# Attention with an MLP behind it: constant bias rows by broadcast DMA, norms put between units, pair loads moved by a slot

## The chip, the cores and the metric

The kernel runs on one core of a Trainium2 chip. A core has TensorE (PE, matmuls), VectorE (DVE), ScalarE (ACT), GpSimd (POOL) and SyncE (SP, which only issues transfers). The metric is the device time of one execution in microseconds, lower is better; it is given as the median of several executions.

## What is computed

Two stages, for 8 batches of 8 heads, 576 positions and head dimension 64:

```python
# attention, per batch and head
cum    = cumsum(max(s, 0))
scores = q @ k.T / 8 + min(-(cum[i] - cum[j]), 0)      # -1e9 above the diagonal
attn_out = softmax(scores) @ v
# the heads side by side give x: [8, 576, 512]
xn  = (x - mean(x)) / sqrt(var(x) + 1e-6) * g_ln
out = x + max(xn @ w_ch1, 0) @ w_ch2                   # 512 -> 2048 -> 512
```

## The kernel before

All instructions stand in one order written out by hand; each engine goes through its own in that order. The main loop runs over the 64 heads, n = 8b + h. `pre(n)` issues loads and casts for later heads. `scores(b, h)` makes the transposed scores of one head in three PSUM banks and ACT's exponentials of them into `er`; `scores_d` does the last 64 keys for two heads at once. `pv_next()` takes the head that is two behind (`pend`) and does `pv`: 15 matmuls into `pot`, then DVE's `rinv`, the product into `xb` and that for the last 64 positions into `xm` (lines 360 to 369).

**Bias as extra rows.** k and q of four heads lie transposed in `kq[i]`, 64 rows of data and four more (rows D to KA): q carries c_hi and three rows of ones, k carries a row of minus ones and c_hi, c_mid, c_lo (`c3`, the scaled cumulative sum in three bf16 pieces). So the score matmul adds the bias. `aug(gam, ...)` writes the c rows of one group of four heads by four small DMAs from `c3` (L197, L199). The constant rows are filled by ACT, POOL and DVE (L538, L552, L608, L611). For head 0 the rows come from small matmuls `ba`, `bb` (L581, L585), since they are needed first.

**How k and q get there.** For the first three batches `qk_pair(g)` transposes pairs of heads on TensorE (L229) and copies them to `kq` by two copies for k and two for q. Pairs come by `ld_cast_pair` (POOL's DMA queue, which casts), or, for pairs 0 and 1, by `ld_pair` on SP and a cast. From batch 3 on, rows are cast by POOL and transposed by DMA. v of a batch comes in five tiles (`ld_v` on SP, `cast_v` on POOL).

**Norm and MLP.** When the last head of a batch has gone through `pv_next`, `ln_aggr`, `ln_xn` (L410, four or five tiles `xn`) and `ln_rstd` follow at once; two heads later `ln_tr` transposes the tiles into `xT` (L426, copy L431). The MLP of a batch is 32 units in a queue: 16 of `mlp1` (512 columns of hidden, four matmuls L439, and a Relu on ACT L449 or DVE L447) and four times four of `mlp2` (four matmuls L457 each; after the fourth, DVE makes `yo`, L466, which SP stores). `run_units(k)` puts k of them between the attention of the heads, so that TensorE has work while ACT and DVE are busy. The last 64 positions of all batches are gathered in `xm`, `xTm` and go through the MLP at the end (`mixed_units`). `keep_warm(k)` puts k matmuls on zeros where TensorE would be idle.

**Pools.** PSUM: `ps_s` three banks for scores, `ps_m` two for units and the first six pairs, `ps_t` two for transposes, later pairs and `scores_d`, `ps_o` one for `pot`. In SBUF, `pairs` holds four pairs, `stage` six tiles of loaded float32.

Of the kernel before, what the change touches and what calls it, by code (L numbers as in the profile page):

```python
# [19 lines left out]
def kernel(  # L20
# [70 lines left out]
    ones = const.tile([BH, S], BF16, name="ones")  # L91
    pick = const.tile([BH, 4, P], BF16, name="pick")
# [107 lines left out]

    def bias_rows():
        tr = ps_t.tile([P, 3, NT, BH], BF16, name="trc", tag="tr")
        for j, src in enumerate((c_hi, c_mid, c_lo)):
            for t in range(NT):
                pn = P if t < NF else TL
                nc.tensor.transpose(
                    tr[0:pn, j, t, :], src[:, t * P : t * P + pn], ident[0:BH, 0:BH]
                )
        for t0, t1, pn in ((0, NF, P), (NF, NT, TL)):
            nc.vector.tensor_copy(  # L210
                out=cT[0:pn, t0:t1, 0, :, 1:4],
                in_=tr[0:pn, :, t0:t1, :].rearrange("p j t x -> p t x j"),
            )
            nc.vector.tensor_copy(out=cT[0:pn, t0:t1, 1, :, 0], in_=tr[0:pn, 0, t0:t1, :])


    def qk_pair(g, k_eng, q_eng):
        b, j = g // 4, g % 4
        i = (g // 2) % 2
        hh = (j % 2) * 2  # L220
        for x, (kind, eng) in enumerate((("k", k_eng), ("q", q_eng))):
            src = ready.pop((kind, g))
            if g < 6:
                tr = ps_m.tile([P, S], BF16, name="trqk", tag="m")
            else:
                tr = ps_t.tile([P, S], BF16, name="trqk", tag="tr")
            for t in range(QT):

                nc.tensor.transpose(  # L229
                    tr[:, t * QP : (t + 1) * QP],  # L230
                    src[0:QP].rearrange("p h c -> p (h c)")[:, t * P : (t + 1) * P],
                    ident[0:QP, 0:QP],
                )
            dst = kq[i][0:D, x, hh : hh + 2, 0:S].rearrange(
                "d u (p r w) -> d u p r w", r=QT // 2, w=2
            )
            for w in range(2):
                copy_on(
                    eng,
                    dst[:, :, :, :, w],  # L240
                    tr[w * D : (w + 1) * D, :].rearrange("d (u r p) -> d u p r", u=2, p=QP),
                )
# [99 lines left out]
    def pv(b, h):  # L342
# [4 lines left out]
        pot = ps_o.tile([P, NT, D + 1], F32, name="pot", tag="pot")  # L347
# [46 lines left out]
    def ln_aggr(b):  # L394
        n = len(x_tiles(b))
        mvs[b] = small.tile([P, 5, 2], F32, name="mv", tag="mv", bufs=2)
        for t in range(n):
            nc.vector.bn_aggr(out=mvs[b][:, t, :], in_=st[b][:, t, :, :])
# [7 lines left out]
    def ln_xn(b):  # L406
        xTs[b] = xtp.tile([P, KD, 512], BF16, name="xT", tag="xT")
        for t, x in enumerate(x_tiles(b)):
            xn = xnp.tile([P, Dm], BF16, name="xn", tag="xn")
            nc.vector.scalar_tensor_tensor(  # L410
                out=xn,
                in0=x,
                scalar=mvs[b][:, t, 0:1],
                in1=gb,
                op0=ALU.subtract,
                op1=ALU.mult,
            )
            xns[b, t] = xn

    def ln_tr(b, t):  # L420
        if (b, t) not in xns:
            return
        xn = xns.pop((b, t))
        tr = ps_t.tile([P, KD, P], BF16, name="trx", tag="tr")
        for kd in range(KD):
            nc.tensor.transpose(tr[:, kd, :], xn[:, kd * P : (kd + 1) * P], ident)  # L426
        if t < NF:
            dst = xTs[b][:, :, t * P : (t + 1) * P]
        else:
            dst = xTm[:, :, (b // 2) * P : (b // 2 + 1) * P]  # L430
        nc.vector.tensor_copy(out=dst, in_=tr)  # L431
# [21 lines left out]
    def mlp2(t, quarter, x, rs, dst):  # L453
        if quarter == 0:
            py[0] = ps_m.tile([P, Dm], F32, name="py", tag="m")
        for fb in range(quarter * 4, quarter * 4 + 4):
            nc.tensor.matmul(  # L457
                py[0],
                lhsT=hT[:, fb, t * P : (t + 1) * P],
                rhs=w2_bf[:, fb, :],  # L460
                start=(fb == 0),
                stop=(fb == FB - 1),
            )
        if quarter == 3:
            yo = yop.tile([P, Dm], F32, name="yo", tag="yo")
            nc.vector.scalar_tensor_tensor(  # L466
                out=yo, in0=py[0], scalar=rs, in1=x, op0=ALU.mult, op1=ALU.add
            )
            dst(yo)


    def chunk_units(xT_of, of_t):
        units = [lambda fb=fb: mlp1(xT_of(), fb) for fb in range(FB)]
        for t in range(NF):
            for qr in range(4):
                units.append(lambda t=t, qr=qr: mlp2(t, qr, *of_t(t)))
        return units

    def batch_units(b):
        def of_t(t):  # L480
            def put(yo):
                nc.sync.dma_start(out=out[b, t * P : (t + 1) * P, :], in_=yo)
# [3 lines left out]
    def mixed_units():  # L486
        def of_t(t):
            def put(yo):
                nc.sync.dma_start(out=out[2 * t, NF * P : S, :], in_=yo[0:TL])
                nc.sync.dma_start(out=out[2 * t + 1, NF * P : S, :], in_=yo[TL:P])  # L490
            return xm[t], rstd[:, 2 * t + 1, NF:NT], put
        return chunk_units(lambda: xTm, of_t)
# [25 lines left out]
    for g in range(2):  # L518
        ld_pair("k", g)
        ld_pair("q", g)  # L520
    for t in range(3):
        ld_v(0, t)
# [9 lines left out]
    for j in range(3):  # L532
# [4 lines left out]
    nc.vector.memset(kq[0][0:KA, 0, :, S:SP], 0.0)  # L537
    nc.scalar.copy(  # L538
        out=kq[0][D:KA, 1, :, 0:S], in_=ones[0:4].unsqueeze(1).to_broadcast([4, G, S])
    )  # L540
# [11 lines left out]
    nc.gpsimd.memset(kq[0][D : D + 1, 0].bitcast(F32), NEG2)  # L552
    ld_cast_pair(2)
# [5 lines left out]

    nc.vector.tensor_scalar(  # L560
# [11 lines left out]
    aug(0, nc.sync, h0=1)  # L572
    ld_v(0, 3)
    qk_pair(0, "dve", "act")
# [3 lines left out]
    for j, src in ((3, ones), (0, c_hi), (1, c_mid), (2, c_lo)):  # L578
        if j == 2:
            keep_warm(4)  # L580
# [12 lines left out]
    cast_pair("k", 1, "pool")  # L593
    cast_pair("q", 1, "pool")
    ld_v(0, 4)
    ld_cast_pair(3)
    v_edges(0)
    for t in range(NT):
        cast_v(0, t, "pool")
    nc.gpsimd.memset(er[TL:P, :, OD : OD + TL], 0.0)  # L600
    nc.gpsimd.memset(er[:, :, OD + TL : EW], 0.0)


    def pre(n):
        if n == 0:
            nc.vector.memset(mhalf, -0.5)
            nc.vector.memset(kq[1][0:KA, 0, :, S:SP], 0.0)
            nc.vector.memset(kq[1][D : D + 1, 0].bitcast(F32), NEG2)  # L608
            ld_w1(0)
        elif n == 1:  # L610
            nc.vector.memset(kq[1][D:KA, 1].bitcast(F32), ONE2)  # L611
            aug(1, nc.sync)
            ld_cast_pair(4)
        elif n == 2:
            nc.sync.dma_start(out=gb, in_=moe_g_ln.partition_broadcast(P))
            ld_w1(1)
        elif n == 3:
            v_edges(1)
        elif n == 4:
            ld_w1(2)  # L620
        elif n == 5:
            ld_cast_pair(5)
        elif n == 6:
            ld_w1(3)
            ld_v(1, 0), ld_v(1, 1), ld_v(1, 2), ld_v(1, 3), ld_v(1, 4)
        elif n == 7:
            ld_w2(0)
        elif n == 8:
            ld_cast_pair(6)
            ld_w2(1)  # L630
            cast_v(1, 0, "pool")
            cast_v(1, 1, "pool")
        elif n == 9:
            ld_w2(2)
            cast_v(1, 2, "pool")
            cast_v(1, 3, "pool")
            cast_v(1, 4, "pool")
        elif n == 10:
            ld_cast_pair(7)
            ld_w2(3)  # L640
        elif n == 13:
            nc.vector.memset(cT[:, :, 0, :, 0], -1.0)
            nc.vector.memset(cT[:, :, 1, :, 1:4], 1.0)
            for r in rows:
                nc.gpsimd.memset(r[:, :, :, KA:P], 0.0)
        elif n == 14:
            bias_rows()

        for g in range(8, 4 * NPE):
            if n == 2 * g - 4:  # L650
                ld_cast_pair(g)
# [25 lines left out]
    NU = {n: 3 for n in range(12, 20)}  # L677

    def pv_next():
# [4 lines left out]
        if ph_ == 7:  # L684
            ln_aggr(pb)
            ln_xn(pb)
            ln_rstd(pb)


    for n in range(BH):  # L690
        b, h = n // H, n % H
        nu = NU.get(n, 4)
        pre(n)
        if n < 10:
# [3 lines left out]
            if n % 2 == 0 and n < 8:  # L698
                g = n // 2 + 1
                qk_pair(g, "dve", "act")  # L700
            if n < 8:
                keep_warm(2)
            if n == 9:
                for t in range(NF):
                    ln_tr(0, t)
                queue += batch_units(0)
            if n > 1 and n != 9:
                pv_next()
            if n == 8:
                pv_next()  # L710
                keep_warm(5)
                qk_pair(5, "act", "act")
            pend.append((b, h))
            continue
        if h % 2 == 1 and n + 1 < NPE * H:
            qk_pair((n + 1) // 2, "act" if h == 1 else "dve", "act")
        scores(b, h)
        run_units(1, True)
        if h % 2 == 0:
            scores_d(b, h // 2)  # L720
        run_units(1)
        pv_next()
        pend.append((b, h))
        lt = {2: (0, 1), 3: (2, 3, 4)}.get(h, ()) if b > 1 else ()
        for t in lt:
            ln_tr(b - 1, t)
            if t != 1 and t != 4:
                run_units(1)
                nu -= 1
        run_units(nu - 2)  # L730
        if b > 1 and h == 3:
            queue += batch_units(b - 1)
# [3 lines left out]
    run_units(5)  # L736
    for t in range(NT):
        ln_tr(B - 1, t)
        run_units(1)
# [33 lines left out]
```

The softmax here doesn't subtract the row's maximum and nothing guards it: scores larger than these inputs give would overflow.

## Time and profile before

| | |
|---|---|
| median of 3 runs | 387.54 us (386.29 to 388.04) |
| the profiled execution | 387.35 us, span 385.7 us |
| PE / DVE / ACT / POOL busy | 363.9 / 202.5 / 194.5 / 161.6 us |
| granted clock, mean | 0.98 |
| moved by DMA | 51.86 MB |
| the largest PE groups | py L457 137.9 us, ph L439 123.2, pot L352 40.6 |
| the idle matmuls of keep_warm | 39, busy 13.9 us |

The span is what the profiler saw between the first and the last instruction; 1.65 us of the execution lie around it. A matmul's end is modelled and runs into the next one, so a busy PE is read as "has work", and a stretch with less busy time than length as one with waits. The page's table of slices gives the busy share of 40 equal stretches of 9.6 us.

### The profile page before, as it was taken

How to read it: one execution, taken by the hardware profiler on the slowest of the kernel's cores; microseconds unless marked ns; L12 is line 12 of the kernel's file. 1: busy time of each engine (PE TensorE's matmuls, PEld its weight loads, DVE VectorE, ACT ScalarE, POOL GpSimd, SP SyncE). 2: the span in 40 equal slices, each digit the busy share in tenths (PEclk: the TensorE clock that was granted, in tenths of full speed). 3: DMA queues.
4: the chain of work that ended last, by engine and by line, in shares of the span. 5: the costliest groups of instructions: out<-in, count | busy, mean ns of one | idle time of the engine just before them, and what ended most of it. 6: DMA issues, size and time to landing. Idle time of an engine off the chain costs nothing.

```text
span 385.7 us, 8249 instructions
## 1 busy us (share of the span) xinstructions
PE 363.9 (94%) x3016; PEld 197.3 (51%) x3016; DVE 202.5 (53%) x538; ACT 194.5 (50%) x366; POOL 161.6 (42%) x442
## 2 busy tenths in 40 slices
PE   7878798997999999999999999999999979999994
PEld 2556455555555555565555555555555534444442
DVE  7557747768644754484356536743665473212211
ACT  7768667673874377427733773376346401411410
POOL 5861377437473365535565563456742110000000
PEclk9889899999999999999999999999999989999999
DMA  8799996178795599759887996589620011002013
GB/s 199 126 182 195 210 168 128 24 167 166 165 186 121 129 229 202 169 132 216 185 202 184 204 191 163 140 200 210 152 97 0 2 56 54 1 29 82 0 34 77
DMA packets 147777, 51.86 MB, mean 134 GB/s; under 512 B 134140, under 2 KB 142936, under 8 KB 147736
## 3 DMA queue, kind: packets, MB, share of 16 engines
q1 hardware_dynamic: 139352, 44.18, 50.5%
q0 software_dynamic: 8384, 7.15, 12.2%
q8 instruction: 24, 0.39, 0.4%
q14 instruction: 17, 0.14, 0.1%
HBM read 37.11 MB, written 9.44 MB: 121 GB/s over the span
## 4 chain that ended last, share of the span: by engine, by line
PE 80%; DMA 8%; DVE 5%; ACT 3%; SPq 1%; issue 1%; POOL 0%; ACTq 0%; DVEq 0%; POOLq 0%
PE py L457 31%; PE ph L439 30%; DMA vtmp<-in_v_dram 7%; PE pot L352 6%; PE sc L276 3%; PE sb L276 3%; PE sa L276 3%; PE trx L426 2%; ACT er L287 2%; DVE xn L410 2%; ACT kq L96 1%; DMA pairtmp<-in_q_dram 1%; PE trqk L229 1%; DMA kq<-c 1%; DVE yo L466 1%
## 5 line engine op out<-in xcount | busy, mean ns | idle before, releaser
L457 PE MATMUL py<-w_bf,hT 128*128 128x512 bf16 x576 | 137.9, 381 | 2.5 <-DVE yo L466 2.2
L439 PE MATMUL ph<-xT,w_bf 128*128 128x512 bf16 x512 | 123.2, 382 | 1.2 <-DVE hT L447 1.0
L449 ACT ACTIVATE hT<-ph 128x512 bf16<-128x512 f32 x107 | 63.9, 598 | 85.5 <-PE ph L439 85.5
L439 PEld LDWEIGHTS <-w_bf 128*128 128x128 bf16 x576 | 52.0, 98 | 55.2 <-issue 6.0
L457 PEld LDWEIGHTS <-hT 128*128 128x128 bf16 x576 | 52.2, 98 | 52.8 <-issue 4.0
L287 ACT ACTIVATE er<-sa 128x512 bf16<-128x512 f32 x64 | 38.1, 596 | 71.6 <-PE sa L276 44.8
L295 POOL TENSOR_SCALAR_AFFINE_SELECT er<-er 128x128 bf16<-128x128 bf16 x216 | 58.4, 294 | 33.3 <-ACT er L287 33.3
L447 DVE TENSOR_SCALAR hT<-ph 128x512 bf16<-128x512 f32 x37 | 25.6, 691 | 58.0 <-PE ph L439 54.9
L163 POOL CAST rows<-rowtmp 128x512 bf16<-128x512 f32 (+1 forms) x50 | 30.4, 607 | 44.3 <-DMA rowtmp<-in_q_dram 39.9
L352 PEld LDWEIGHTS <-er 128*128 128x128 bf16 x960 | 38.3, 99 | 17.9 <-DVE xm L369 3.1
L276 PEld LDWEIGHTS <-kq 68*128 68x128 bf16 x440 | 32.8, 98 | 27.6 <-DMA kq<-c 2.5
L360 DVE RECIPROCAL rinv<-pot 128x5 f32<-128x5 f32 x64 | 12.4, 194 | 61.5 <-PE pot L352 61.3
L352 PE MATMUL pot<-v_bf,er 128*128 128x65 bf16 x960 | 40.6, 195 | 2.3 <-DVE xm L369 1.8
L287 ACT ACTIVATE er<-sc 128x512 bf16<-128x512 f32 x64 | 39.1, 611 | 0.0
L100 POOL CAST v_bf<-vtmp 128x512 bf16<-128x512 f32 (+1 forms) x40 | 24.6, 620 | 32.9 <-DMA vtmp<-in_v_dram 32.5
L287 ACT ACTIVATE er<-sb 128x512 bf16<-128x512 f32 x64 | 38.3, 598 | 0.0
L466 DVE SCALAR_TENSOR_TENSOR yo<-py,rstd,xb 128x512 f32<-128x512 f32 x32 | 23.8, 748 | 25.5 <-PE py L457 20.3
L96 ACT COPY kq<-trqk 64x576 bf16<-64x576 bf16 x28 | 22.5, 802 | 11.9 <-PE trqk L229 11.7
L362 DVE TENSOR_TENSOR xb<-pot,rinv 128x256 f32<-128x256 f32 x64 | 27.2, 425 | 2.2
L276 PE MATMUL sa<-kq 68*128 68x512 bf16 x64 | 24.6, 385 | 3.0 <-DMA kq<-c 2.4
L276 PE MATMUL sc<-kq 68*128 68x256 bf16 (+1 forms) x208 | 25.2, 232 | 0.2
L386 DVE BATCH_NORM_STATS2 stats<-xb 128x6 f32<-128x128 f32 (+1 forms) x96 | 25.0, 320 | 0.4
(93 smaller groups left out, 302.2 us busy)
## 6 DMA issues: line engine op xcount, KB each, us to landing
vtmp<-in_v_dram SPq DMA_DIRECT2D x32, 256.0 KB
out_dram<-yo SPq DMA_DIRECT2D x32, 256.0 KB
rowtmp<-in_k_dram SPq DMA_DIRECT2D x40, 128.0 KB
rowtmp<-in_q_dram SPq DMA_DIRECT2D x40, 128.0 KB
w_bf<-in_moe_w_ch_dram POOLq DMA_DIRECT2D x8, 512.0 KB, 11.1
kp<-in_k_dram POOLq DMA_DIRECT2D x10, 144.0 KB, 4.4
qp<-in_q_dram POOLq DMA_DIRECT2D x10, 144.0 KB, 5.1
vtmp<-in_v_dram SPq DMA_DIRECT2D x8, 128.0 KB
```

The source lines that it names most:

```text
L96: nc.scalar.copy(out=out, in_=in_)
L163: nc.gpsimd.tensor_copy(out=r[0:pn, :, :, 0:D], in_=loaded.pop(("rows", gam, t))[0:pn])
L276: nc.tensor.matmul(a[:, c + a0 - q0 : c + a1 - q0], lhsT=k_cols(b, h, kb), rhs=cols, start=True, stop=not (pe_mask and diag),)
L287: nc.scalar.activation(out=e[:, o : o + 512], in_=a, func=ACT.Exp, scale=scale)
L295: nc.gpsimd.affine_select(out=e[:, o : o + P], in_=e[:, o : o + P], compare_op=ALU.is_ge, fill=0.0, base=0, pattern=[[1, P]], channel_mult ...
L352: nc.tensor.matmul(pot[:, t, :], lhsT=e[:, o : o + P], rhs=vv[:, kb, h, :], start=(kb == 0), stop=(kb == last),)
L362: nc.vector.tensor_tensor(out=xb[b][:, :, hs], in0=pot[:, 0:NF, 0:D], in1=rinv[:, 0:NF].unsqueeze(2).to_broadcast([P, NF, D]), op=ALU.mult,)
L439: nc.tensor.matmul(ph, lhsT=w1_bf[:, kd, fb * P : (fb + 1) * P], rhs=xT[:, kd, :], start=(kd == 0), stop=(kd == KD - 1),)
L447: nc.vector.tensor_scalar_max(out=hT[:, fb, :], in0=ph, scalar1=0.0)
L449: nc.scalar.activation(out=hT[:, fb, :], in_=ph, func=ACT.Relu)
L457: nc.tensor.matmul(py[0], lhsT=hT[:, fb, t * P : (t + 1) * P], rhs=w2_bf[:, fb, :], start=(fb == 0), stop=(fb == FB - 1),)
L466: nc.vector.scalar_tensor_tensor(out=yo, in0=py[0], scalar=rs, in1=x, op0=ALU.mult, op1=ALU.add)
```

## The change

It has these parts:

- **Constant rows.** A new `constant_rows(i, h0)` fills the ones and minus rows of `kq[i]` by two broadcast DMAs on SP from small tiles; the copies and memsets on ACT, POOL and DVE go. Rows and `aug(1)` are issued ahead of the loop.
- **Loads of the first batch.** Pair 1 is loaded with a cast through POOL's queue; v tiles 0 and 1 come after the first constant rows, tile 2 after `aug(0)`, tiles 3 and 4 and `gb` after `aug(1)`. POOL's memsets of v_bf and er come ahead of its loads.
- **Pair loads and pairs.** Pair 5 is loaded at n = 6 instead of 5, pair 6 at 9 instead of 8 (behind the five casts of v of batch 1, which are all at n = 9), pair 7 at 11 instead of 10, w1 parts 2 and 3 and v of batch 1 a slot or two earlier. Pairs 9 and 11 come one slot earlier than before, pair 10 two. Pairs are transposed at n = 11, 13, 14, 15, 16 and 21 instead of 11, 13, 15, 17, 19 and 21. `qk_pair` gives each of its four copies an engine of its own.
- **Norms.** `ln_aggr` and `ln_xn` of all tiles become one `ln_xn(b, t)` per tile. Tile 0 follows the last pv, tiles 1 to 4 are put at h = 1, 2, 3, 3 of the next batch; transposes at h = 2, 2, 3, 3, 4.
- **Units.** For batch 0, six units run at n = 9, ahead of n = 10. The number of units per head is worked out so that the queue of a batch is empty at h = 3 of the next but one.
- **Small ones.** Four idle matmuls ahead of `ba`'s last part go, and two later ones. Half of the copies of `bias_rows` move to ACT, and it runs at n = 12. pv of head 7 of batch 0 uses `ps_m`. The last tile of all is made in two halves of 256 columns, and one of the two stores of a mixed tile is issued by ACT.

```diff
+    def constant_rows(i, h0=0):
+        for x, src, r0, m, a in ((1, ones, D + 1, 3, 0), (0, minus, D, 1, h0)):
+            nc.sync.dma_start(
+                out=kq[i][r0 : r0 + m, x, a:G, 0:S],
+                in_=src[0:m, :].unsqueeze(1).to_broadcast([m, G - a, S]),
+            )
...
-    def ln_aggr(b):
-        n = len(x_tiles(b))
+    def ln_open(b):
         mvs[b] = small.tile([P, 5, 2], F32, name="mv", tag="mv", bufs=2)
-        for t in range(n):
-            nc.vector.bn_aggr(out=mvs[b][:, t, :], in_=st[b][:, t, :, :])
+        xTs[b] = xtp.tile([P, KD, 512], BF16, name="xT", tag="xT")
...
+    def ln_xn(b, t):
+        tiles = x_tiles(b)
+        if t >= len(tiles):
+            return
+        nc.vector.bn_aggr(out=mvs[b][:, t, :], in_=st[b][:, t, :, :])
...
+        if t == len(tiles) - 1:
+            ln_rstd(b)
...
-    for g in range(2):
-        ld_pair("k", g)
-        ld_pair("q", g)
-    for t in range(3):
-        ld_v(0, t)
+    ld_pair("k", 0)
+    ld_pair("q", 0)
...
-    nc.scalar.copy(
-        out=kq[0][D:KA, 1, :, 0:S], in_=ones[0:4].unsqueeze(1).to_broadcast([4, G, S])
-    )
+    nc.vector.memset(minus.bitcast(F32), NEG2)
...
+    constant_rows(0, 1)
+    ld_v(0, 0)
+    ld_v(0, 1)
...
+    ld_cast_pair(1)
...
     aug(0, nc.sync, h0=1)
+    ld_v(0, 2)
+    constant_rows(1)
+    aug(1, nc.sync)
     ld_v(0, 3)
-    qk_pair(0, "dve", "act")
+    ld_v(0, 4)
+    nc.sync.dma_start(out=gb, in_=moe_g_ln.partition_broadcast(P))
+    qk_pair(0, ("act", "act"), ("act", "dve"))
...
-        if j == 2:
-            keep_warm(4)
...
+    PAIR_LOADS = {12: 8, 13: 9, 14: 10, 17: 11}
+    PAIRS = {11: 6, 13: 7, 14: 8, 15: 9, 16: 10, 21: 11}
...
         elif n == 5:
+            ld_v(1, 0), ld_v(1, 1), ld_v(1, 2), ld_v(1, 3), ld_v(1, 4)
+        elif n == 6:
             ld_cast_pair(5)
...
+        elif n == 9:
+            for t in range(NT):
+                cast_v(1, t, "pool")
             ld_cast_pair(6)
...
             if n == 8:
                 pv_next()
-                keep_warm(5)
-                qk_pair(5, "act", "act")
+                for t in range(1, NF):
+                    ln_xn(0, t)
+                keep_warm(3)
+            if n == 9:
+                for t in range(NF):
+                    ln_tr(0, t, "act")
+                queue += batch_units(0)
+                run_units(4)
+                qk_pair(5, ("dve", "dve"), ("act", "act"))
+                run_units(2)
...
+        end = next(m for m in (8 * i + 3 for i in range(2, B + 1)) if m >= n)
+        nu = -(-len(queue) // (end - n + 1)) - 2
+        if n in PAIRS:
+            qk_pair(PAIRS[n], ("dve", "dve"), ("act", "act"))
+        ln = b > 1
         scores(b, h)
         run_units(1, True)
         if h % 2 == 0:
             scores_d(b, h // 2)
+        if ln and h in (2, 3, 4):
+            ln_tr(b - 1, (0, 2, 4)[h - 2])
         run_units(1)
         pv_next()
         pend.append((b, h))
...
+        if ln and h in (1, 2, 3):
+            ln_xn(b - 1, h)
+            run_units(1)
+            nu -= 1
+        if ln and h in (2, 3):
+            ln_tr(b - 1, (1, 3)[h - 2])
+        if ln and h == 3:
+            ln_xn(b - 1, 4)
+        run_units(nu)
         if b > 1 and h == 3:
+            run_units(len(queue))
             queue += batch_units(b - 1)
...
-    run_units(5)
+    run_units(2)
     for t in range(NT):
+        ln_xn(B - 1, t + 1)
+        run_units(1)
         ln_tr(B - 1, t)
-        run_units(1)
```

The split of the last tile and ACT's store:

```diff
+            halves = ((0, 256), (256, 512)) if last and t == NF - 1 else ((0, 512),)
+            for c in halves:
...
-                nc.sync.dma_start(out=out[2 * t + 1, NF * P : S, :], in_=yo[TL:P])
+                nc.scalar.dma_start(out=out[2 * t + 1, NF * P : S, c0:c1], in_=yo[TL:P])
```

## The prediction

> **What bounds the kernel now.** I read the page's busy shares first, then the engine table by stages, then TensorE's waits, then the order of time around single waits. "Unit" below means one piece of the MLP, four matmuls of 512 columns, 0.865 us (1.73 us for eight in the chain of waits). n counts heads from 0: n = 8b + h.
>
> ```profile
> PE 363.9 (94%) x3016; PEld 197.3 (51%) x3016; DVE 202.5 (53%) x538; ACT 194.5 (50%) x366; POOL 161.6 (42%) x442
> ...
> PEclk9889899999999999999999999999999989999999
> ```
> ```profile
> 34.00:48.00 14.00, 9.97 (x115) 6.36 (x115) 10.40 (x35) 9.93 (x19) 3.76 (x5) 0.92 1.23 204
> 60.00:72.00 12.00, 10.74 (x112) 6.25 (x109) 10.37 (x25) 7.36 (x14) 7.35 (x19) 1.00 0.46 78
> 84.00:96.00 12.00, 9.69 (x99) 5.83 (x98) 10.12 (x30) 5.70 (x11) 7.96 (x21) 1.00 0.81 172
> 148.00:186.00 38.00, 38.00 (x342) 21.26 (x341) 21.37 (x62) 19.95 (x41) 19.17 (x58) 1.00 0.78 180
> 300.00:324.40 24.40, 22.15 (x154) 11.53 (x153) 13.48 (x39) 3.84 (x7) 2.28 (x5) 0.93 0.09 34
> ```
> Columns: stretch, length, busy PE, weight load, DVE, ACT, POOL, granted clock, DMA share, GB/s. From 97 to 300 us TensorE never stops. Idle time lies in the first 96 us and at 300 to 324. In the busy stretch, whatever makes TensorE wait is paid in full.
>
> ```profile
> PE sa L276 <- DMA kq<-c: 2.4, 1, 2.4
> PE py L457 <- DVE yo L466: 2.2, 1, 2.2
> PE trqk L229 <- DVE xT L431: 2.1, 1, 2.1
> ```
> The first is at n=4: the bias rows of kq[1] (four DMAs of aug(1), held on SP until DVE's memset L611) land late. The other two are the norm bursts of batches 7 and 1, where five xn of 0.74 us run back to back on DVE.
>
> ```profile
> 22.00:25.40 3.40, 1.00 (x14) 1.00 1.19 178
> 25.40:28.80 3.40, 3.40 (x39) 0.50 1.14 189
> ```
> After a stretch with TensorE busy for 1.00 of 3.40 us, the next one runs at half clock. The same stands at 42.5 (1.72 busy) and 312.1 (1.15), but not at 86.8 (1.99).
>
> ```profile
> 169.68 0.62 PE L352 MATMUL pot<-v_bf,er 128*128 128x65 bf16 x15
> 170.14 0.39 PE L426 MATMUL trx<-ident,xn 128*128 128x128 bf16 x4
> 170.34 0.19 DVE L360 RECIPROCAL rinv<-pot 128x5 f32<-128x5 f32 x1 [0.90 <-PE pot L352]
> 170.36 1.03 PE L457 MATMUL py<-w_bf,hT 128*128 128x512 bf16 x4
> 170.57 0.42 DVE L362 TENSOR_TENSOR xb<-pot,rinv 128x256 f32<-128x256 f32 x1
> 170.91 0.27 DVE L369 TENSOR_SCALAR xm<-pot,rinv 64x64 f32<-64x64 f32 x1
> 171.10 0.97 DVE L431 COPY xT<-trx 128x512 bf16<-128x512 bf16 x2
> ```
> This is h=3 of a steady batch. The attention matmuls end for TensorE at 170.14 (call it X). DVE is done with their eviction at 171.10, X+0.96, while TensorE has already gone on: the transposes need an xn made a head and a half earlier, so they never wait.
>
> **The Trainium skill.** "TensorE: Matmul & The Clock Gate", Part 1, says that an idle window of about 3.4 us halves the clock for the next; the rows above agree, down to windows that are only half idle. "DMA: Bandwidth & Descriptors", Queues, rings and completion order, says that each DMA engine takes turns between queues, packet by packet. The trace agrees: the v loads of batch 1 (256-byte rows) needed up to 7.2 us each to be issued beside the weights. The same page, Rules for kernel authors, says that an outer dimension of c < 16 keeps a DMA on at most c engines; this concerns the new constant rows (3 partitions and 1), and no run here shows it.
>
> **The change, part by part.** The sum is made against the profiled execution (387.35 us, span 385.7); the median of the three runs, 387.54, is 0.2 above it. A plus is time won.
>
> *Constant rows.* Out go ACT's copy L538 (2.11 us), POOL's memset L552 (1.16) and DVE's L608 and L611 (1.12 each). In come four SP DMAs, about 0.57 us of issue each (row kq<-c), the first two ahead of v tile 0, and a 0.3 us memset that ends before DVE's first wait at 3.79. ACT's copy was hidden (its first cast waited for the pair load until 4.96). aug(1) moves from 17.6 to about 11, so its rows land near 15, against 21 when n=4 wants them. The 2.40 us wait goes, and the half clock after it; next late there is ACT's exponentials. Four idle matmuls (1.66 us, at 8.14) leave the way of bias row c_lo: its eviction L588 starts at 9.3 instead of 10.4, bounded next by DVE's quarter of qk_pair(0). The first scores start at 11.3 instead of 12.0. Lead at n=8: 0.7 + 2.4 + 0.9 (ACT's waits of 0.66 and 0.23 in the slow window) = about 4 us.
>
> *Loads.* Pair 1 comes in by POOL's queue instead of SP plus POOL casts. v tiles 2 to 4 are issued behind aug(0), constant rows and aug(1), until about 14.6; their casts end near 17.2, and POOL issues w1 part 0 at 17.2, as before. What comes behind decides n=11: POOL now waits for all five v casts of batch 1 *before* it issues pair 6, and n=11 begins with pair 6's transposes. Before, w1, w2 parts 0 and 1 and pairs 4 to 6 took from 17.2 to 47.3 (29.82 + 17.5 to landing). Without pair 6 (2.1 us, between landings at 41.7 and 43.8) and without gb beside them, they end at 43.7 to 45.2; v, which takes turns with them, follows some 2 us later as before (47.3 to 49.2): 45.7 to 47.2. Pair 6: cast 0.65, two issues 0.65 each, 4.0 to landing: 50.5 to 52.
>
> *Units before the first wait on v.* Norms of batch 0: stats end at about 35.4, four times aggr+xn (0.18 + 0.74) to 39.2, last copy (ACT now, estimated 0.6 from its 512-wide rows) 40.1. In a half-clock window to 42.5, four units end at 45. Then qk_pair(5) holds both ps_m buffers for its copies (DVE 1.6, ACT 1.6): units 5 and 6 at 46.8 to 48.5, scores(10), two units, pv(1,0), one unit: 52.2; pair 6's transposes 0.5; scores of n=11 at 52.9, with 9 units done. Before: at 52.21, with 4 done. Five units are 4.3 us, less 0.7: **+3.6**.
>
> *n=11 to 16.* Before, 27.3 us from 52.2 to 79.5 held 25.4 of work (19 units, 6 scores at 0.66, 6 pv at 0.45, transposes), so 1.9 was lost. After, DVE's memsets of cT (0.35 + 0.86, now at n=11) and the copies delay a Relu by about 0.4; pair 7 comes behind two more w2 parts (near 60.5, wanted at 61.7). Four pairs in a row cost ACT 1.6 each, but units are past their Relus by then. I keep 0.9 lost: **+1.0**.
>
> *Norms of batch 1.* The unit queue is planned to be empty at n=19, so transposes there have no unit beside them. Three waits: 0.55 (tile 0: xn at X+2.95 against TensorE at X+2.45), 0.2, and 2.0 (tile 3: nothing between pv and transposes); a chance of 0.4 on a half-clock window, 1.7 us: 3.4 in all. Before 3.2 (17.2 us for 14.05 of work): **-0.2**.
>
> *Norms of batches 2 to 6.* At h=3 xn of tile 3 is put behind pv's eviction, with one unit before its transposes. xn ends at X + 0.96 + 0.18 + 0.05 + 0.74 = X+1.93, TensorE is there at X+0.87, and starts at X+2.0: 1.1 us, five times, in a stretch with no idle time: **-5.5**. Bounds: 0.6 (DVE gets to the eviction sooner) to 1.4 (a yo of 0.75 in between) per batch. Tiles 0, 1, 2 and 4 have at least three units between (tile 0 by 0.3 us), and wait for nothing.
>
> *Norm of batch 7.* The burst is cut up. From pv's end at 307.9: 13 units (11.25), five transposes (1.2), waits of 0.4, 0.6, 0.25, 0.25, 0.9: 322.7, against 324.3: **+1.6** (0.8 to 2.4).
>
> *Tail.* The last tile goes in two halves: yo 0.42 instead of 0.75, and the second of the two last stores on ACT's queue beside the first instead of 0.52 behind: **+0.85**. Thirty-two matmuls of 256 columns cost what sixteen of 512 do. Stores on ACT wait for yo, but no Relu is behind them.
>
> *Moved at no cost.* pv of (0,7) in ps_m (its 0.93 wait goes, DVE's norm chain covers it); bias_rows at n=12, half of its copies on ACT (0.72, 0.27); the rows memset on POOL at n=16, with casts behind it a head from use; k0's copies on ACT.
>
> Sum: 3.6 + 1.0 - 0.2 - 5.5 + 1.6 + 0.85 = 1.35 us won: 386.0 profiled, **386.2** as a median.
>
> **Rivals.**
> *Same, as summed* (0.50; own range 384 to 388.5). A measurement tells about 0.5% (1.9 us) from no change. Of this case 0.17 lie below 385.6.
> *Faster: the wait at h=3 is short.* If DVE needs X+1.3 only, five waits of 0.4 cost 2.0: 382.7. For it: DVE idles 0.90 ahead of the eviction. Against: the eviction cannot start before pv ends. 0.17.
> *Slower: pair 6 comes late at n=11.* If the last v tile of batch 1 lands at 49.2 as before, pair 6 lands at 54.5 and the scores start at 55.0: 2.1, and 3 us idle bring a half-clock window, 1.7: 390.0. It decides from v landing later than 47.0, which is within my 45.7 to 47.2. For it: POOL's order. Against: less traffic ahead. 0.27, of which 0.25 slower.
> *The later pair loads change nothing*, because POOL's issues ran far ahead of TensorE anyway (weights issued at 17 to 24 for n=9 on): then only norms and tail count, and front units are won without pair 6's wait; about 387. 0.06.
>
> **The numbers.** Faster 0.17 + 0.17 = 0.34, slower 0.25 and 0.02 for a longer wait at h=3, 0.27, same 0.39. The range runs from the short-wait case to the late pair with its half window: 382 to 390.5.
>
> **What would show it.** TensorE's waits: kq<-c gone; trx <- DVE xn about 1.1 us in each of five batches and 2.0 near 90 us. The steady batch takes 38.9 us instead of 37.8. Scores of n=11 at 52 to 53.5 with nine units before it. A steady stretch still at 38.0 of 38.0 busy would prove me wrong on the largest term; a wait on DMA qp at n=11 means the slow rival.

## The result and the profile after

The changed kernel takes **393.08 us** (391.73 to 394.19, 4 runs) against 387.79 us of the kernel before on the same chip: the ratio is 1.014, with an interval of 1.009 to 1.018. It is slower by some 5 us, where the forecast was 386.2 us, no clear change. Some executions of a kernel run in a slower state: medians and ranges here are over all runs, ratios and their intervals over the fast runs alone. The profiled execution took 393.09 us, its span 391.4 us, 5.7 us more than before.

The page first: the busy shares and the granted clock of the kernel after, in 40 slices of 9.8 us.

```profile
PE 361.5 (92%) x2974; PEld 197.4 (50%) x3026; DVE 207.4 (53%) x534; ACT 193.4 (49%) x369; POOL 162.5 (42%) x441
...
PE   7996699987999899989998999899989989999995
...
PEclk8599899999999999999999999999999999999999
```

TensorE has the same work, but for six idle matmuls, and a longer span. The row of busy tenths, which stood at 9 all through the middle before, now dips to 8 once in every four slices, that is once a batch. The clock has lost its dip at the end (the long norm of batch 7 is gone) and got a deeper one at the start. The stages give the sizes (columns as before: stretch, length, busy PE, weight load, DVE, ACT, POOL, granted clock, DMA share, GB/s):

```profile
34.00:48.00 14.00, 9.78 (x79) 4.99 (x76) 7.13 (x23) 7.47 (x15) 2.87 (x4) 0.88 1.16 193
84.00:96.00 12.00, 8.46 (x95) 5.26 (x95) 10.52 (x30) 3.70 (x8) 7.29 (x19) 1.00 0.85 191
148.00:186.00 38.00, 36.69 (x329) 20.59 (x333) 22.17 (x62) 18.78 (x39) 20.39 (x57) 1.00 0.85 168
300.00:324.40 24.40, 23.05 (x190) 11.75 (x190) 16.85 (x48) 8.84 (x17) 3.32 (x12) 1.00 0.03 12
```

A steady 38 us, full before, now has 1.3 us of waiting in it; the stage of batch 1's norms (84 to 96) went from 9.69 to 8.46 busy. TensorE's waits of the kernel after (total, times, longest) say on what:

```profile
PE trx L438 <- DVE xn L420: 13.7, 14, 2.1
PE pot L362 <- DVE xm L379: 1.6, 3, 0.9
```

The wait on `kq<-c` at n = 4 (2.4 us before) is gone, and no pair is waited for at n = 11. In their place stands one line of 13.7 us. Of its 14 waits, four (2.99 us) lie in batch 0's norms, two in batch 1's (1.23 and 2.14), three in batch 7's (1.62). The other five are one per steady batch: 1.23, 1.00, 1.23, 1.00 and 1.23, together 5.69 us. This is one of them in the order of time, at h = 3 (start, length, engine, line, operation, in brackets what ended the idle time before it):

```profile
133.07 0.63 PE L362 MATMUL pot<-v_bf,er 128*128 128x65 bf16 x15
...
133.53 1.03 PE L469 MATMUL py<-w_bf,hT 128*128 128x512 bf16 x4
133.73 0.20 DVE L370 RECIPROCAL rinv<-pot 128x5 f32<-128x5 f32 x1 [0.90 <-PE pot L362]
133.96 0.42 DVE L372 TENSOR_TENSOR xb<-pot,rinv 128x256 f32<-128x256 f32 x1
134.40 0.29 DVE L379 TENSOR_SCALAR xm<-pot,rinv 64x64 f32<-64x64 f32 x1
...
134.71 0.24 DVE L418 BATCH_NORM_AGGREGATE mv<-stats 128x2 f32<-128x18 f32 x1
134.98 0.75 DVE L420 SCALAR_TENSOR_TENSOR xn<-xb,mv,gb 128x512 bf16<-128x512 f32 x1
...
135.79 0.40 PE L438 MATMUL trx<-ident,xn 128*128 128x128 bf16 x4 [1.23 <-DVE xn L420]
```

TensorE leaves the attention at 133.53 (the prediction's X) and does one unit. DVE first stands idle for 0.90 us, waiting for pv, then evicts it, and only then makes the tile that TensorE wants next. The transposes start at X+2.26. (The 1.23 us in brackets are counted from the modelled end of the unit, 1.03 us after its start. A unit with other work behind it is followed 0.87 us after its start, so this break costs 1.39 us from start to start.)

One more loss is read from the clock, in windows of 3.4 us of the kernel after:

```profile
14.40:17.80 3.40, 3.18 (x21) 2.02 (x20) 1.60 (x2) 2.67 (x6) 1.17 (x2) 0.52 0.58 148
38.30:41.70 3.40, 1.38 (x13) 0.83 (x14) 2.10 (x6) 2.12 (x4) 1.08 (x2) 0.98 1.22 195
41.70:45.10 3.40, 3.40 (x9) 1.22 (x8) 0.00 (x0) 0.60 (x1) 1.17 (x2) 0.52 1.21 198
92.90:96.30 3.40, 1.34 (x11) 0.89 (x13) 2.80 (x9) 0.81 (x3) 1.11 (x5) 0.98 0.83 214
96.30:99.70 3.40, 3.40 (x20) 1.75 (x20) 1.47 (x4) 1.25 (x4) 2.87 (x6) 0.52 1.13 224
```

In this execution the clock was half in three windows in a row from 7.5 to 17.8 (the first row is the third of them), and in one each behind the norms of batch 0 and of batch 1. The last one starts soon after the wait of 2.14 us and costs half of 3.4, 1.7 us.

**Where the 5.7 us are.** Marks are the first MLP unit of each batch. Before, the five intervals from batch 1's to batch 6's are 38.51, 37.95, 37.73, 37.95 and 37.73 us; after, 41.75, 38.90, 39.35, 38.90 and 39.47: 8.5 us longer. Up to the first mark the kernel after is 0.95 us ahead (95.79 against 96.74), it wins 1.58 us in batch 7's norm (36.09 against 37.67) and 0.24 from there to the end. 8.5 - 0.95 - 1.58 - 0.24 = 5.7.

### The profile page after: what moved, and what is told of

Same layout as the page of the kernel before. It is cut to its first block, busy times and chain, and to the rows that moved or that the text cites. A ratio compares the mean times of both kernels' runs of the same rounds, so it can differ in the third digit from the quotient of the medians.

```text
span 391.4 us, 8208 instructions
## 1 busy us (share of the span) xinstructions
PE 361.5 (92%) x2974; PEld 197.4 (50%) x3026; DVE 207.4 (53%) x534; ACT 193.4 (49%) x369; POOL 162.5 (42%) x441
## 4 chain that ended last, share of the span: by engine, by line
PE 68%; DVE 11%; DMA 9%; SPq 3%; issue 3%; ACT 3%; POOL 2%; ACTq 0%; POOLq 0%
PE ph L451 28%; PE py L469 23%; PE pot L362 5%; DMA vtmp<-in_v_dram 4%; PE sa L285 3%; PE sc L285 3%; PE sb L285 3%; DVE xn L420 2%; SPq L152 2%; DMA rowtmp<-in_q_dram 1%; DMA rowtmp<-in_k_dram 1%; DVE xb L372 1%; PE trx L438 1%; DVE stats L396 1%; DMA kq<-c 1%
## 5 line engine op out<-in xcount | busy, mean ns | idle before, releaser
L469 PE MATMUL py<-w_bf,hT 128*128 128x512 bf16 (+1 forms) x564 | 133.7, 373 | 1.2
L469 PEld LDWEIGHTS <-hT 128*128 128x128 bf16 x592 | 53.0, 98 | 47.0 <-issue 0.2
L304 POOL TENSOR_SCALAR_AFFINE_SELECT er<-er 128x128 bf16<-128x128 bf16 x216 | 60.0, 299 | 39.1 <-ACT er L296 38.8
L164 POOL CAST rows<-rowtmp 128x512 bf16<-128x512 f32 (+1 forms) x50 | 32.2, 644 | 36.0 <-DMA rowtmp<-in_q_dram 35.4
L362 PEld LDWEIGHTS <-er 128*128 128x128 bf16 x960 | 37.5, 98 | 16.5 <-DVE xm L379 2.4
L362 PE MATMUL pot<-v_bf,er 128*128 128x65 bf16 x960 | 39.6, 194 | 1.6 <-DVE xm L379 1.6
L99 DVE COPY kq<-trqk 64x576 bf16<-64x576 bf16 x23 | 18.4, 802 | 16.8 <-PE trqk L238 15.8
L438 PE MATMUL trx<-ident,xn 128*128 128x128 bf16 x144 | 14.3, 223 | 13.8 <-DVE xn L420 13.7
```

The costliest lines, as they stand in the source:

```text
L164: nc.gpsimd.tensor_copy(out=r[0:pn, :, :, 0:D], in_=loaded.pop(("rows", gam, t))[0:pn])
L304: nc.gpsimd.affine_select(out=e[:, o : o + P], in_=e[:, o : o + P], compare_op=ALU.is_ge, fill=0.0, base=0, pattern=[[1, P]], channel_mult ...
L362: nc.tensor.matmul(pot[:, t, :], lhsT=e[:, o : o + P], rhs=vv[:, kb, h, :], start=(kb == 0), stop=(kb == last),)
L469: nc.tensor.matmul(py[0], lhsT=hT[:, fb, t * P : (t + 1) * P], rhs=w2_bf[:, fb, c0:c1], start=(fb == 0), stop=(fb == FB - 1),)
```

## The experiments

My theory after the result: the loss is the place of tile 3's `xn` on DVE, behind pv's eviction, and nothing else in the change is slower than before. Rivals: the front, with its half clock, loses; or cutting the norms into tiles costs by itself, because DVE's work then lies across every head. The kernels of the first four runs had 387.61 us of before beside them, the next four 387.98, the last four 388.07.

**e1_xn3_early: only the order on DVE.** The kernel after, with one call ahead of `pv_next()`:

```diff
+        if ln and h == 3:
+            ln_xn(b - 1, h)
         pv_next()
...
         if ln and h in (1, 2, 3):
-            ln_xn(b - 1, h)
+            if h < 3:
+                ln_xn(b - 1, h)
```

> The changed kernel with one move: at h = 3 the norm of tile 3 (aggr and xn) stands ahead of the pv instead of behind it. Theory (place of tile 3): the five waits of trx on xn of 1.0 to 1.23 us in batches 2 to 6 go, the 2.14 us wait near 95 us shrinks to about 1, and with it the half-clock window behind it may go (1.7 us): 393.1 - 5.7 - 1.1 - 0 to 1.7 = 384.5 to 386.5 us; the steady batch takes 37.7 to 38.0 us. Rival (the time is lost in the loads, pairs and unit plan of the first 96 us): within 1 us of 393.1.

Measured: **383.92 us** (382.83 to 385.56), ratio to before 0.990 [0.987, 0.994], a little below the expected range. One moved call wins 9 us against the kernel after, and beats the kernel before. The same place in its order of time:

```profile
131.99 0.75 DVE L420 SCALAR_TENSOR_TENSOR xn<-xb,mv,gb 128x512 bf16<-128x512 f32 x1
132.05 0.63 PE L362 MATMUL pot<-v_bf,er 128*128 128x65 bf16 x15
...
132.51 1.03 PE L469 MATMUL py<-w_bf,hT 128*128 128x512 bf16 x4
...
132.72 0.19 DVE L370 RECIPROCAL rinv<-pot 128x5 f32<-128x5 f32 x1
...
133.38 0.39 PE L438 MATMUL trx<-ident,xn 128*128 128x128 bf16 x4
```

`xn` now fills DVE's idle time ahead of the eviction. The eviction isn't held up: 0.67 us behind pot's start, 0.66 without. The transposes have no wait in brackets. The waits and the stretch agree:

```profile
PE trx L438 <- DVE xn L420: 6.7, 9, 1.4
```
```profile
148.00:186.00 38.00, 38.00 (x342) 21.22 (x340) 22.42 (x62) 19.82 (x41) 21.36 (x62) 1.00 0.87 191
```

The wait line falls by five times and 7 us. Its marks are 38.70, 37.73, 38.08, 37.73 and 37.95 us apart, 190.2 in all against 198.4: with the waits the time around them goes too, and in this run the half window behind batch 1, where the wait is 1.39 now.

**e2_norms_only and e11_norms_mended: the norm part alone.** e2 is the kernel before with only the norms of the change; e11 is e2 with the edit of e1.

> The kernel before with the norm part of the change alone: ln_xn per tile, put at h = 1, 2, 3, 3, transposes at h = 2, 2, 3, 3, 4, and the end loop of the change. Loads, constant rows, pairs, unit plan and tail as before. Theory (place of tile 3): five waits of 1.0 to 1.2 us appear in batches 2 to 6, about 1.1 in batch 1 in place of the burst (2.3), and the end gains 1.6: 387.8 + 5.7 - 1.2 - 1.6 = 390.7 us (389.5 to 392.5). Rival: within 1 us of 387.8, or faster by the two bursts, 384.

Measured: 393.24 us (392.64 to 395.85), ratio 1.013 [1.011, 1.016], the whole loss of the change and more than the range expected. Steady batches take 39.1 to 39.4 us, and it waits on `xn` as the kernel after does (1.23 to 1.65 us in each of batches 2 to 6):

```profile
PE trx L428 <- DVE xn L410: 10.0, 11, 1.7
```

> The kernel before with only the norm part of the change, as in e2_norms_only, but with xn of tile 3 ahead of pv_next() at h = 3. Theory (the norm part's loss is tile 3's place and nothing else): the five steady waits go, batch 7 wins 1.6 us, batch 1 keeps some 1.3 us of its wait: 387.0 to 388.5 us against 387.9 of before, steady batches 37.7 to 38.0 us. Rival (cutting the norms up costs by itself, by DVE's work lying across pv's evictions in every head): 389.5 to 391, steady batches of 38.3 us or more.

Measured: 385.85 us (384.84 to 388.15, 11 runs), ratio 0.995 [0.992, 0.998], better than the range expected. Its waits:

```profile
PE sa L276 <- DMA kq<-c: 2.4, 1, 2.4
PE trx L428 <- DVE xn L410: 2.2, 4, 0.7
```

Steady batches are back at 37.7 to 38.0 us, batch 7 takes 36.08, and the wait on `kq<-c` at n = 4 shows that this is the old front. So cutting up the norms costs nothing in itself; that rival is out. Put rightly, the norm part wins about 2 us by itself.

e11 also has no wait on `xn` near 95 us, where e1 keeps one of 1.39. There, at n = 19, the unit plan of before has a unit left between pv and the transposes of tile 3:

```profile
93.39 0.63 PE L352 MATMUL pot<-v_bf,er 128*128 128x65 bf16 x15
93.85 1.03 PE L459 MATMUL py<-w_bf,hT 128*128 128x512 bf16 x4
94.72 0.39 PE L428 MATMUL trx<-ident,xn 128*128 128x128 bf16 x4
```

In e1, with the plan of the change, the queue is empty by then and pv is followed by the transposes. DVE is late in e11 too, at another place: pair 10's transposes wait 1.28 us for one of its copies at 90.5 us.

**e4_norms_back: all the rest.** The kernel after with the norms of before.

> The changed kernel with the norms of before: all aggr and xn at once behind the last pv of a batch, transposes at h = 2 and 3, and the end loop of before; loads, constant rows, pairs, unit plan and tail of the change stay. Theory (place of tile 3): the five waits go (5.7 us), batch 1 has its burst again (about equal to its 3.4 us of waits and half of a window), the end loses 1.6: 393.1 - 5.7 + 1.6 = 389.0 us (387.5 to 390). Rival (loads, pairs, unit plan cost the time): 393 or more.

Measured: 385.10 us (380.88 to 387.04, 4 runs), ratio 0.989 [0.983, 0.996], below the range expected. The front does not lose, so that rival is out too. How much the rest wins is measured roughly: 1.5 to 6.7 us by the interval, 2.5 by the medians, where the prediction had 3.6 + 1.0 + 0.85 = 5.45. On top of the mended norms it wins less: e1 against e11 (ratios 0.990 and 0.995) is 1.7 us. On top of the norms as the change has them it wins nothing: 393.08 us against the 393.24 of e2.

So the parts don't add up. Batch 1 shows one place where the lead is lost: at n = 19 e2 has a unit in the gap, waits 1.00 us on `xn`, and its clock stays full; the kernel after has none, waits 2.14, and a half window of 1.7 us follows. That this is all of the difference is not shown.

**e7_two_units: a smaller dose.** The kernel after, with both units of h = 3 between pv and the transposes of tile 3, so that TensorE comes there 0.87 us later.

> The changed kernel, xn of tile 3 still behind the pv at h = 3, but with both units of that head ahead of the transposes of tile 3 instead of one. A dose: with one unit (0.87 us) TensorE waits 1.0 to 1.23, with two it should wait 0.15 to 0.35, and the first unit of h = 4 may wait 0.2 longer for the copy. Theory: 0.7 to 0.85 us back per batch, five times, 393.1 - 3.5 to 4.3 = 388.8 to 389.6 (1.7 less if the half-clock window near 97 us goes too). Rival (not the distance but DVE's load as such): 392.5 or more.

Measured: 390.34 us (388.41 to 394.36, 19 runs), ratio 1.006 [1.004, 1.008]: 2.7 us won of the 3.5 to 4.3 expected. The steady waits are down to 0.36, 0.13, 0.54, 0.13 and 0.36 us, and the last four intervals alternate (38.17, 38.99, 38.17, 38.81). The dose moves the time the right way. The rest of the loss is traced: the same four intervals are 37.73 and 37.95 us in turn in e9, whose waits there are gone. The interval of 38.99 us holds the wait of 0.54, the 0.16 us by which a unit's modelled end lies behind the place where the next work could have started, and 0.30 more where the first unit of h = 4 waits for DVE's copy of tile 3 (it starts 0.53 us behind the start of the scores' last part, 0.23 in e1). The expectation named that last wait at 0.2.

**e3_warm4: the four idle matmuls back** ahead of `ba`'s last part.

> The changed kernel with the four idle matmuls ahead of the last part of ba put back. The profile after shows TensorE at half clock from about 7 to 17 us where before had it from 8.3 to 11.7. Theory (clock): the idle matmuls kept the windows busy; with them back half clock ends near 11 us, the scores of n = 2 start near 16.5 instead of 18.0, n = 4 near 21 instead of 22.5. If this lead reaches n = 11 the time is 391.9 us; if DVE's norm chain at n = 8 or the queue of batch 0 takes it up, 393.1 with scores of n = 11 still at 54.5 to 55. Rival (phase of the clock windows by chance): half clock to 17 us again.

Measured: 393.39 us (392.42 to 394.13), ratio 1.014 [1.012, 1.017], the same as the kernel after. In its profiled run the early half clock was gone and the scores of n = 2 started at 16.87 us, against 17.99, and those of n = 11 at 53.79, against 54.87. Three of its four runs had a mean granted clock of 0.991, against 0.972 to 0.978 in the kernel after, and still the median is no lower; where that lead goes is left open. Whether a half window falls in the front depends on more than these matmuls: e5 doesn't have them either, and its scores of n = 2 start at 16.57.

**e5_plan: a place for the last wait.** e1, with the unit queue planned one head longer for batch 0, so that two units are left at n = 19:

```diff
         end = next(m for m in (8 * i + 3 for i in range(2, B + 1)) if m >= n)
+        end += end == 19
```

> e1_xn3_early with another unit plan for batch 0: its 26 units are spread up to n = 20 on paper, so that two are left for n = 19, between whose transposes e1 had none. Theory (no unit beside the transposes at n = 19): the wait of trx on xn near 95 us (1.39 in e1) falls under 0.4; 383.9 - 1.0 to 1.4 = 382.5 to 382.9. Rival (DVE's chain sets the time there whatever TensorE has to do): the two units only move, the wait goes elsewhere, 383.9.

Measured: **383.34 us** (382.91 to 383.69), ratio 0.989 [0.985, 0.993], not to be told from e1. The wait stayed, 1.31 us:

```profile
91.20 0.62 PE L362 MATMUL pot<-v_bf,er 128*128 128x65 bf16 x15
93.14 0.40 PE L438 MATMUL trx<-ident,xn 128*128 128x128 bf16 x4 [1.31 <-DVE xn L420]
```

But both units that the plan left for n = 19 run ahead of pv, and none stands between it and the transposes of tile 3. So this edit doesn't test whether a unit there would hide the wait; e11, which has one there, has no such wait.

**e9_xn3_h2: tile 3 a head earlier still.** As e5, with tile 3's `xn` at h = 2 and tile 4's ahead of pv at h = 3.

> As e5_plan (tile 3's xn ahead of pv, units left for n = 19), but xn of tile 3 made a head earlier still, at h = 2 behind the transposes of tile 1, and xn of tile 4 ahead of pv at h = 3. Theory (each wait on xn is only a matter of DVE's order): the wait of about 1.3 us near 95 us, which two kernels kept, goes, and with it the last wait on xn before the final batch: 382.0 to 383.5 us, steady batches 37.7 to 37.9 us each. Rival (at batch 1 DVE is short of time, whatever its order, since yo, stats and copies of two batches meet there): the wait moves to another of DVE's results, 383 to 384.5, and may come up in steady batches too.

Measured: 383.80 us (382.63 to 386.61, 6 runs), ratio 0.989 [0.987, 0.992]. The wait on `xn` near 95 us went, and this one came at the next head's first unit (one of 0.65 us on tile 0 stays at 87.6):

```profile
PE ph L451 <- DVE xT L99: 1.9, 1, 1.9
```

The rival held: here it is the copy of the last tile, behind pv's eviction in DVE's order, that the first MLP unit waits for. The steady batches stay at 37.7 to 38.0.

**e6_warm_norm and e8_ps_t: the front's other waits.** e6 is e1 with two idle matmuls behind each of the first three transposes of batch 0's norms, against the half clock there. e8 is e1 with pair 5 transposed in `ps_t` (`if g < 5`), so that it doesn't take both `ps_m` buffers from the units at n = 9.

> e1_xn3_early with two idle matmuls behind each of the first three transposes of batch 0's norm at n = 9, where TensorE waits 0.3 to 1.4 us for DVE four times. Theory (half clock): the window before 40 us counts as busy, half clock at 40 to 45 us goes, the first four units take 3.5 to 4 us instead of 5.1 to 5.5, and 1.2 to 1.6 us reach n = 11: 382.3 to 382.7. Rival (POOL's and DVE's copies hold the units): 383.9, and if the idle matmuls delay transposes, up to 384.5.

> e1_xn3_early with pair 5 transposed into ps_t instead of ps_m. At n = 9 both ps_m buffers are held by pair 5 until its copies on DVE and ACT (1.6 us each) are done: waits of 0.43 and 0.95 us ahead of units 4 and 5. Theory (these waits lie on the path to n = 11): they go, scores of n = 11 come 1.0 to 1.4 us earlier with the same nine units done, 382.5 to 382.9. Rival: v of batch 1 and pair 6 land only just in time, the gain turns into a wait for them, 383.5 to 383.9.

Measured: e6 384.85 us (382.59 to 387.86, 10 runs), ratio 0.993 [0.989, 0.997]; e8 385.06 us (381.78 to 388.05, 13 runs), ratio 0.991 [0.988, 0.994]. Both did in the trace what they were to do: from the scores of n = 9 to those of n = 10 it is 13.7 us in e6 and 14.0 in e8, against 15.7 in e1, and the waits on `ps_m` are gone in e8. Neither median is lower than e1's. The time up to n = 8 differs from one profiled run to another by more than this (19.8 to 24.1 us from n = 0, among the kernels with the front of the change). In e8's 13 runs the mean granted clock ranged from 0.965 to 0.991, and the three runs at 0.991 took 381.8 to 383.6 us, the one at 0.965 took 388.05. What these two edits are worth is left open.

**e10_loads_back: the pair loads of the title.** e5 with pairs 5, 6 and 7 loaded a slot earlier, as they were before.

> As e5_plan, but the loads of pairs 5, 6 and 7 one slot earlier, as they were before the change (5 at n = 5 behind the v loads, 6 at n = 8 ahead of the casts of v, 7 at n = 10). Theory (pair loads are far ahead of their use in either order, no wait on pairs was seen): the same as e5_plan within 1 us, 382.5 to 384.5, no wait on qp or kp. Rival (pair 6 ahead of v's casts takes the transfers that v and w2 want, or POOL gets to v's casts later): pot or py at n = 10 to 12 waits, 385 to 386.

Measured: 383.67 us (382.82 to 385.95, 6 runs), ratio 0.991 [0.988, 0.994], the same as e5. One wait of 0.94 us at n = 9 is put down to pair 5's load here; in e5 the same one, of 0.95, is put down to the copy of pair 5, which holds the `ps_m` buffer. No other wait on a pair's load stands there. The later slot of the pair loads makes no difference that these runs show.

**e12_aug_first: what the first head waits for.** e5 with v tiles 0 and 1 loaded behind `aug(0)`, not ahead of it:

```diff
     constant_rows(0, 1)
-    ld_v(0, 0)
-    ld_v(0, 1)
...
     aug(0, nc.sync, h0=1)
+    ld_v(0, 0)
+    ld_v(0, 1)
     ld_v(0, 2)
```

> As e5_plan, but v tiles 0 and 1 are loaded behind aug(0) on SP instead of ahead of it. Theory (aug(0) lands at about 13.9 us only because the v rows lie ahead of it, and head 0's last scores wait 0.6 to 1.25 us for it): that wait goes, head 0 ends about 1 us earlier, and pv of head 0 at n = 2 waits for v instead, 0 to 1 us: 382.3 to 383.8 us. Rival (v is what n = 2 to 4 need first): pot waits for v_bf 2 us or more, and a half-clock stretch comes behind it: 385 to 386.5.

Measured: 387.08 us (384.46 to 391.25, 22 runs), ratio 0.997 [0.995, 0.999], slower than e5 by some 3 us (3.1 by the ratios, 3.7 by the medians). The wait of head 0 on `kq<-c` goes (its next scores start at 13.27 us, against 14.52 in e5), and in its place comes:

```profile
PE pot L362 <- POOL v_bf L101: 3.2, 2, 1.7
```

The rival held, with more than its price. That a half-clock stretch makes up the rest is not shown: its profiled run, of 385.6 us, is faster than its median.

The lowest medians are those of e5, e10, e9 and e1, which these runs can't tell apart, nor, by the intervals, from e4, e6 and e8. These four beat both kernels, by about 1% the kernel before and by 2.4% the one after.

## Why the prediction was wrong

By its steps, each against the profiled execution (plus is time won):

| step | predicted | found |
|---|---|---|
| front, to the scores of n = 11 | +3.6 | +1.7 |
| n = 11 to 16 | +1.0 | -0.7 |
| norms of batch 1 | -0.2 | about 0, and -1.7 for the half window behind them |
| norms of batches 2 to 6 | -5.5 | -6.8 |
| norm of batch 7 | +1.6 | +1.58 |
| tail | +0.85 | +0.24 |
| sum | +1.35 | -5.7 |

The largest loss and its place were forecast rightly. What failed is the balance: the front and n = 11 to 16 were to win 4.6 us and won 1.0, the half window behind batch 1 was counted at 0.4 of its 1.7 us, and the loss of batches 2 to 6 was put 1.3 too low.

**The norms of batches 2 to 6: the right mechanism, price too low.** The prediction had TensorE there at X+0.87 and the start of the transposes at X+2.0, 1.1 us per batch. In two batches they did start near X+2.0; in the other three at X+2.26, since eviction and `aggr` took longer (in the one shown `xn` starts at X+1.45, not X+1.19). Less 0.87 each, that is 6.5 us from start to start, of which the waits in brackets show 5.69. The last 0.3 of the 6.8 stays untraced. The rival "the wait at h = 3 is short" reckoned with 0.4 per batch; the shortest was 1.00. e1, e2 and e11 show that tile 3's place in the order makes the slowdown: e2 brings it in alone, and the one move takes it away in both kernels.

**The front: the step that failed most in the trace.** The scores of n = 11 start at 54.87 us, not 52.9, with the nine units done: five units (4.33 us) less 2.66 is 1.7. The wait of 2.4 us at n = 4 went, but three things ate into the lead. *First*, the half clock from 7.5 to 17.8 us: the scores of n = 0 start 0.98 us earlier than before, those of n = 1 0.80 later. *Second*, `aug(0)` landed no earlier (its wait ends at 13.86 us, 13.92 before). *Third*, n = 9 had a window of half clock up to 45.1 us, where the prediction let it end at 42.5, and the units then waited for `ps_m` and its copies (0.43 and 0.95 us; e8 shows these go with another bank).

How much of this is chance of the windows? The Trainium skill, "TensorE: Matmul & The Clock Gate", Part 1, says that the window is free-running, so that the same kernel meets it at different points. The runs agree: e1 and e5 have the same code up to n = 9, and the first score matmul of n = 1 took 0.63 us in e1's profiled run, at 16.23, and 0.38 in e5's, at 14.52. So a lead of 1 to 2 us that rests on one execution's windows is not one to count on as a median. With the norms put right the rest wins 1.7 us (e1 against e11); by itself it wins 1.5 to 6.7 (e4), so for the rest alone 5.45 us is not excluded.

**n = 11 to 16.** The prediction expected 0.9 us lost there instead of 1.9. The stretch took 26.75 us for 17 units, against 27.80 for 19. Two units less are 1.73, and one pair more ahead of n = 17 is 0.51 (its transposes start at 69.03, the scores behind them at 69.54), which comes to 26.58: it wasted 0.2 us more than before, and won nothing. The wait of 1.0 us on a Relu of DVE stands in both kernels. The pair that came in here left the next stretch, so batch 1's norms, about even in the table, cost some 0.5 us more than before by themselves.

**Norms of batch 1.** The waits of 0.55, 0.2 and 2.0 us came as 1.23, 0.12 and 2.14, and the half window that had a chance of 0.4 came in the profiled run. **Batch 7** came out as worked: three waits of 0.50, 0.45 and 0.67 us, and five transposes between units. **The tail** is shorter by 0.45 us from the mixed tiles' first unit on, less 0.21 in batch 7's MLP. The last `yo` took 0.48 us instead of 0.75, so 0.27 of the 0.33 came. The second queue let the last two stores be issued together, and their issues ended 0.83 us earlier after the mixed tiles' first unit, as summed; but the last packet came 1.79 us behind them, where it was 1.43 before.

**The rivals.** "Pair 6 late at n = 11" gave a time near the measured one (390.0), but is refuted: no wait on a pair stands at n = 11, and e10 moves the loads without effect. "The later pair loads change nothing" had its premise right and its sum wrong. The chance of slower (0.27) hung on pair 6. It should have come from the sum itself: one well-founded loss of 5.5 us that recurs in every batch stood against gains of 5.45 us in the front and tail, each of which needed several waits to vanish at once.

## What to carry to other kernels

When an engine's work is cut up and spread through an order written by hand, ask for each piece what it stands behind: the same 0.75 us on DVE is free in the idle time ahead of an eviction and costs over 1 us of TensorE right behind it, and the trace of before showed that gap (0.90 us). Ask too what the waiting engine has left to do there: at batch 1 one unit more in the gap took the wait on `xn` away (e11). Weigh a loss that recurs in a full stage more than gains in a starved one: where several things are late together, taking one away mostly brings up the next. And where much meets, as at batch 1's norms, moving one instruction may only move the wait, as it did in e9.

## What was not expected of the hardware

In the kernel after, the granted clock stayed half for three windows in a row (7.5 to 17.8 us) though the profile has TensorE busy for 3.31 of 3.4, 2.77 of 3.5 and 3.18 of 3.4 us in them (with ends that are modelled). Windows of 1.38 and 1.34 us busy out of 3.4 were each followed by half clock.

The mean granted clock of a run doesn't show all of it. For e6's profiled run the profile gives 1.00 all through, from 7.4 to 17.7 us too, but the first score matmuls of n = 0, 1 and 2 (11.60, 16.07 and 18.63 us) took 0.63 us, as at half clock in e1, and that of n = 3 took 0.38. So these means compare runs only roughly. The runs of one kernel, e8, spread over 6.3 us.
